# A fixed order of work in a token mix: first loads earlier, additions in pairs, outputs in one step

## The chip, the core and the metric

The kernel runs on one core of one Trainium2 chip. The metric is the device time of one execution in microseconds (us), from the runs of the kernel, with the program and its inputs unchanged between runs. One execution was also taken by the hardware profiler; its own time and its span stand in the table below.

Five engines work side by side, each through its own instructions in order: PE (matrix products), DVE (vector work), ACT (activations and copies), POOL (some copies, and one of the queues of DMA transfers) and SP (the main queue of DMA transfers). An instruction waits until the semaphores that it names have been raised by others; everything behind it on its engine waits with it.

## What is computed

The input is a sparse attention over 4 batches, 8 heads, 768 positions of 64 features, in blocks of 32 positions: each block of queries sees its neighbours, the first and the last block, and three sampled blocks; the first and the last block of queries see everything. Its result goes, heads side by side, as `x` (4 x 768 x 512) into a token mix:

```python
theta = x @ w_theta
cos_t, sin_t = (np.cos(theta), np.sin(theta))
zr = x * cos_t
zi = x * sin_t
yr = np.einsum('ts,bsd->btd', w_tok_r, zr)
yi = np.einsum('ts,bsd->btd', w_tok_i, zi)
y = yr + yi
u = x + y
return (u + np.maximum(u @ w_ch, 0.0)).astype(np.float32)
```

The weights come as 64-bit numbers and are decoded on the chip into a high and a low part (`w_theta_hi`, `w_ch_lo` and so on). Each product of two such values is made as three matrix products: high by high, high by low, low by high.

## The kernel before, in words

**Attention** (`attention`, up to about 290 us) runs over 56 units, one step of an outer loop for each; a unit is one block of queries of two batches with all heads (for the first and the last block: with a third of the keys). A step of that loop makes the scores of the next unit (L315, S), their maxima (L323, m), the exponentials (L341, P), transposes (L351, T; copied out at L357, pT), and the products with the values (L373, X) of the unit before, which DVE divides by their sums (L381 to L384, xo). SP stores the result to `xs` in DRAM (L400). The keys of a unit stand in `kg` (two places), its values in `va` and `vb`, its queries in `q` (four places, one for two units). Batches 0 and 1 of the mix are in the first half of `xs`, which attention has finished long before its last units.

**The mix** (`token_mix`) is a generator. Attention calls it in its last units, so that the first steps of the mix lie between them; the rest follows behind attention. The order inside is written out by hand and nothing reorders it: each engine gets its instructions as the code issues them. A step `k` of the mix takes 128 positions of one batch, six steps (`j` = 0 to 5) make a batch, 24 steps the whole. For a step there are:

- `load_raw` (L541) reads x of the step from `xs` into `xr` through SP's queue, `turn` (L553) transposes it on DVE into `xT`, `high` and `low` (L557 on ACT, L561 on DVE) split it, `theta` (L568 to L571) makes 12 products of 512 columns on PE;
- `integer` (L577, L578 on ACT) and `reduce` (L584 to L586 on DVE) bring the angle into range, `sines` (L592 to L594 on ACT) make cosine and sine, `load` (L535) reads x again as `xa`, in four transfers, `times` (L602 on DVE) multiplies, `split` (L609 on ACT, L610 on DVE) makes high and low parts `zh` and `zl`;
- `mix` (L627) makes 48 products: four groups `c` of 128 channels, each with a part of 512 positions in a bank of its own (`ya`, four banks) and a part of 256 positions; two groups share the bank of their smaller parts (`yb`, two banks);
- at `j` = 5 `add_x` (L642 on DVE) adds x to y, ACT copies the high part `uh` (L644) and DVE makes the low part `ul` (L645);
- the eight outputs of a batch (`out`, two column parts for each of four groups `e`; 12 products each at L651 to L653, sums in the two buffers of `ps_h`, which theta uses as well) are made in the middle of the mix of the next batch's steps `j` = 1 and `j` = 2, four in each; `finish` (L657 on DVE, into one of the two buffers `o`) adds, and L658 stores;
- the outputs of the last batch have no next step: `outs_at_the_end` makes them with sums in the banks of `ya` and `yb`, again two groups in one bank.

Step `k` issues, ahead of its own mix, theta of step `k`+2, sines, times and split of `k`+1, and turn, high and low of `k`+3. In the first eight steps pieces of the last weights are decoded as well, 14 in all by the list `shares`: a piece is ACT L62, DVE L67 to L77, ACT L80 (the high part), DVE L84 and L85 (the low part), and its raw words come through POOL's queue (L58) into one of two buffers. The last eight pieces are `w_ch`, the weights of the outputs.

SBUF places are taken by pools: the pools of the mix's later part (`xp` for xa, `tz` for sines, the decoder's, `zp` and so on) lie over those of attention, and the first write to a place waits for the last reader of what stood there. The bottom pool of attention is `gp`, which holds kg, va and vb together.

Of the kernel before, what the change touches and what calls it, by code (L numbers as in the profile page):

```python
# [19 lines left out]
P = 128  # L20
# [155 lines left out]
def attention(tc, qT, qE, kT, vr, sampled, xs, ident, early_pieces, late_pieces, first_place, follow):  # L176
# [13 lines left out]
    with ExitStack() as ctx, ExitStack() as early:  # L190
# [4 lines left out]
        ps_s = [early_s.enter_context(tc.tile_pool(name=f"ps_s{x}", bufs=1, space=PSUM, side="right")) for x in range(2)]  # L195
        gp = ctx.enter_context(tc.tile_pool(name="gp", bufs=1))
# [11 lines left out]
        kgs = [gp.tile([P, 8, 8, 32], F32, name=f"kg{x}") for x in range(2)]  # L208
# [223 lines left out]

        with tc.manual_schedule():
# [17 lines left out]
            for n in range(steps):  # L451
# [46 lines left out]
                if len(units) - 4 <= n < len(units):  # L498
                    next(follow)
# [3 lines left out]
def token_mix(tc, w, last_pieces, xs, outT, bias, nb):  # L503
# [11 lines left out]
    with ExitStack() as late, ExitStack() as ctx:  # L515
        tps = [ctx.enter_context(tc.tile_pool(name="tp0", bufs=1, side="right"))]
        hp = ctx.enter_context(tc.tile_pool(name="hp", bufs=2, side="right"))
        rp = ctx.enter_context(tc.tile_pool(name="rp", bufs=2, side="right"))
        ap = ctx.enter_context(tc.tile_pool(name="ap", bufs=1, side="right"))

# [92 lines left out]
        def mix(k, between):  # L613
# [4 lines left out]
            for c in range(4):  # L618
# [12 lines left out]
                if j == 5:  # L631
                    add_x(b, c)
# [4 lines left out]
        def add_x(b, c):  # L637
            if b not in us:
                us[b] = [up.tile([P, 4, 768], F32R, tag=f"u{x}", name=f"u{x}{b}") for x in "hl"]
            u = xT[b][:, c, :]  # L640
            for (t0, n), acc in zip(halves, ys[b][c]):
                nc.vector.tensor_tensor(u[:, t0 : t0 + n], acc, u[:, t0 : t0 + n], op=ALU.add)  # L642
            uh, ul = [t[:, c, :] for t in us[b]]
            nc.scalar.copy(uh, u)  # L644
            nc.vector.tensor_tensor(ul, u, uh.bitcast(F32), op=ALU.subtract)  # L645
# [9 lines left out]
        def finish(b, e, t0, n, ps, queue):  # L655
            o = wk.tile([P, 512], F32, tag="o", name=f"of{b}_{e}_{t0}")[:, :n]
            nc.vector.scalar_tensor_tensor(o, ps, 0.0, xT[b][:, e, t0 : t0 + n], op0=ALU.max, op1=ALU.add)  # L657
            queue.dma_start(outT[b, 128 * e : 128 * e + 128, t0 : t0 + n], o)  # L658

        def out(b, e, half):  # L660
            t0, n = half
            ps = ps_h.tile([P, 512], F32, tag="h", name=f"o{b}_{e}_{t0}")[:, :n]
            for c in range(4):
                channels(b, c, e, t0, n, ps, c == 0, c == 3)
            finish(b, e, t0, n, ps, nc.sync)

        def outs_at_the_end(b):
# [19 lines left out]
        load_raw(2)  # L687
# [27 lines left out]
        with tc.manual_schedule():  # L715
# [59 lines left out]
def sparse_attention_then_token_mix(ctx, tc, qT, qE, kT, vr, sampled, w_theta, w_tok_r, w_tok_i, w_ch, outT):  # L775
# [57 lines left out]
    follow = token_mix(tc, w, last, xs, outT, bias, n_batch)  # L833
    attention(tc, qT, qE, kT, vr, sampled.bitcast(I32), xs, ident, early, late, first_place, follow)
# [49 lines left out]
```

## Time and profile before

| what | us |
|---|---|
| runs of the kernel | 670.45, 670.45, 675.64 (median 670.45) |
| the profiled execution, its own time | 673.61 |
| its span, first to last instruction | 671.8 |
| PE busy | 564.7 (84%) |
| DVE busy | 425.7 (63%) |
| ACT busy | 327.3 (49%) |
| POOL busy | 148.2 (22%) |
| mean granted clock of PE | 0.946 of full speed |

In a timeline or chain row the first number is the start from the span's begin, the second the duration, both in us, then engine, line and operation; "x4" counts merged instructions; a bracket gives the idle time of the engine before it and what ended it. In a list of waits the three numbers are the total in us, how many times, and the longest. A matmul starts when the row says, but its duration reaches past the start of the next one: the distance between starts is what it takes.

### The profile page before, as it was taken

How to read it: one execution, taken by the hardware profiler on the slowest of the kernel's cores; microseconds unless marked ns; L12 is line 12 of the kernel's file. 1: busy time of each engine (PE TensorE's matmuls, PEld its weight loads, DVE VectorE, ACT ScalarE, POOL GpSimd, SP SyncE). 2: the span in 40 equal slices, each digit the busy share in tenths (PEclk: the TensorE clock that was granted, in tenths of full speed). 3: DMA queues.
4: the chain of work that ended last, by engine and by line, in shares of the span. 5: the costliest groups of instructions: out<-in, count | busy, mean ns of one | idle time of the engine just before them, and what ended most of it. 6: DMA issues, size and time to landing. Idle time of an engine off the chain costs nothing.

```text
span 671.8 us, 18527 instructions
## 1 busy us (share of the span) xinstructions
PE 564.7 (84%) x7648; PEld 443.5 (66%) x7648; DVE 425.7 (63%) x959; ACT 327.3 (49%) x660; POOL 148.2 (22%) x252
## 2 busy tenths in 40 slices
PE   2877666777878778779997978998999997999994
PEld 1554444555645456558886767887788886888873
DVE  4677657567899769649988784445743647543242
ACT  1866567556777758556554542243523344431110
POOL 1267445450396446130000000000000000000000
PEclk9988899889999889798998997998999999999998
DMA  8938999866789878642332122111111210111002
GB/s 321 302 91 239 283 269 260 234 181 237 220 234 283 242 214 251 183 126 80 90 94 79 33 77 78 66 47 33 35 67 63 72 47 18 46 48 48 0 1 94
DMA packets 57108, 90.47 MB, mean 135 GB/s; under 512 B 5696, under 2 KB 37568, under 8 KB 56640
## 3 DMA queue, kind: packets, MB, share of 16 engines
q1 hardware_dynamic: 47168, 57.02, 28.2%
q0 software_dynamic: 6688, 21.78, 12.2%
q10 hardware_dynamic: 3168, 10.49, 5.2%
q8 instruction: 60, 0.98, 0.6%
q14 instruction: 24, 0.20, 0.1%
HBM read 76.68 MB, written 12.58 MB: 133 GB/s over the span
## 4 chain that ended last, share of the span: by engine, by line
PE 50%; DVE 14%; DMA 3%; ACT 3%; issue 2%; POOL 0%; DVEq 0%; SPq 0%; ACTq 0%
PE ya L627 18%; PE yb L627 9%; PE h L568 3%; PE h L569 3%; PE h L571 3%; PE o L651 2%; PE o L652 2%; PE o L653 2%; DVE m L323 2%; DVE xT L642 2%; PE X L373 2%; PE S L315 1%; PE T L351 1%; DMA va<-in_vr_dram 1%; DMA xr<-xs 1%
## 5 line engine op out<-in xcount | busy, mean ns | idle before, releaser
L627 PE MATMUL ya<-w_second,zh 128*128 128x512 f32 x288 | 110.0, 404 | 0.0
L627 PE MATMUL yb<-w_second,zh 128*128 128x256 f32 x288 | 83.0, 288 | 14.8 <-DVE xT L642 14.8
L341 ACT ACTIVATE P<-S,nm 128x256 f32<-128x256 f32 x176 | 69.2, 480 | 16.8 <-DVE nm L325 15.9
L357 ACT COPY pT<-T 128x512 f32<-128x512 f32 x88 | 47.8, 591 | 48.3 <-PE T L351 46.8
L315 PE MATMUL S<-kg,q 64*32 64x256 f32 x1408 | 59.0, 412 | 14.7 <-issue 12.8
L323 DVE TENSOR_REDUCE m<-S 128x2 f32<-128x512 f32 x88 | 56.4, 683 | 20.7 <-PE S L315 20.6
L627 PEld LDWEIGHTS yb<-w_second,zh 128*128 128x128 f32 x288 | 56.0, 194 | 17.8 <-DVE xT L642 17.3
L373 PE MATMUL X<-va,pT 128*32 128x65 f32 (+1 forms) x1408 | 50.2, 234 | 20.3 <-issue 12.8
L351 PE MATMUL T<-ident,P 128*128 128x128 f32 x352 | 59.0, 299 | 8.7 <-ACT P L341 3.7
L627 PEld LDWEIGHTS ya<-w_second,zh 128*128 128x128 f32 x288 | 55.7, 193 | 13.9
L351 PEld LDWEIGHTS T<-ident,P 128*128 128x128 f32 x352 | 41.5, 148 | 33.4 <-ACT P L341 21.0
L627 PE MATMUL ya<-w_second,zl 128*128 128x512 f32 x144 | 58.9, 409 | 0.0
L373 PEld LDWEIGHTS X<-va,pT 128*32 128x32 f32 (+1 forms) x1408 | 35.8, 116 | 29.8 <-issue 18.4
L294 POOL DMA_INDIRECT vb<-in_vr_dram,rows x44 | 47.2, 1074 | 36.0 <-PE X_w L373 28.3
L373 PE MATMUL X<-vb,pT 128*32 128x65 f32 (+1 forms) x1408 | 49.9, 232 | 3.0 <-issue 3.0
L584 DVE SCALAR_TENSOR_TENSOR rr<-t,h 128x512 f32<-128x512 f32 x24 | 16.5, 688 | 45.1 <-ACT t L578 45.1
L315 PEld LDWEIGHTS S<-kg,q 64*32 64x32 f32 x1408 | 24.2, 112 | 31.2 <-issue 21.0
L373 PEld LDWEIGHTS X<-vb,pT 128*32 128x32 f32 (+1 forms) x1408 | 37.9, 117 | 5.5 <-issue 5.5
L627 PE MATMUL yb<-w_second,zl 128*128 128x256 f32 x144 | 41.3, 287 | 0.0
L627 PE MATMUL ya<-w_first,zh 128*128 128x512 f32 x96 | 36.9, 408 | 4.6 <-ACT zh L609 4.6
L657 DVE SCALAR_TENSOR_TENSOR of<-o,xT 128x512 f32<-128x512 f32 (+1 forms) x24 | 13.3, 558 | 43.4 <-PE o L653 43.4
L568 PE MATMUL h<-w_theta_hi,xh 128*128 128x512 f32 x96 | 39.3, 409 | 1.6 <-ACT xh L557 1.6
(165 smaller groups left out, 1280.4 us busy)
## 6 DMA issues: line engine op xcount, KB each, us to landing
va<-in_vr_dram SPq DMA_DIRECT2D x30, 260.0 KB
xr<-xs SPq DMA_DIRECT2D x24, 256.0 KB
q<-in_qT_dram SPq DMA_DIRECT2D x22, 256.0 KB
xs<-xo SPq DMA_DIRECT2D x44, 128.0 KB
xa<-xs SPq DMA_DIRECT2D x88, 64.0 KB
raw_tok_r<-in_w_tok_r_dram ACTq DMA_DIRECT2D x8, 576.0 KB
out_dram<-of SPq DMA_DIRECT2D x16, 256.0 KB
va<-in_vr_dram SPq DMA_DIRECT2D x30, 130.0 KB
```

The costliest lines, as they stand in the source:

```text
L294: nc.gpsimd.indirect_dma_start(out=vb[0:96], out_offset=None, in_=vr, in_offset=bass.IndirectOffsetOnAxis(ap=tab.rows[:, bp, i : i + 1], a ...
L315: nc.tensor.matmul(sc[32 * p : 32 * p + 32, e, b, :], q[rows, b, p, :], keys[rows, :, 4 * b + p, :], start=True, stop=True)
L323: nc.vector.tensor_reduce(m[:, 2 * e : 2 * e + 2], sc[:, e], axis=AX.X, op=ALU.max)
L341: nc.scalar.activation(pt[:, e, b], sc[:, e, b], AF.Exp, bias=nm[:, 2 * e + b : 2 * e + b + 1], scale=0.125)
L351: nc.tensor.transpose(banks[k // 4][:, k % 4], pt[:, (k // 2) % 2, k % 2, 128 * (k // 4) : 128 * (k // 4) + 128], ident)
L357: nc.scalar.copy(out[:, 4 * h : 4 * h + 4], bank)
L373: nc.tensor.matmul(s["X"][32 * p : 32 * p + 32, b, e, :], s["T"][0:rows, 4 * c + 2 * e + b, 32 * p : 32 * p + 32], v[0:rows, v0 : v0 + 65] ...
L568: nc.tensor.matmul(ps, hi[:, c, :], wh[:, c, :], start=c == 0, stop=False)
L569: nc.tensor.matmul(ps, hi[:, c, :], wl[:, c, :], start=False, stop=False)
L571: nc.tensor.matmul(ps, lo[:, c, :], wh[:, c, :], start=False, stop=c == 3)
L584: nc.vector.scalar_tensor_tensor(r, t, -C1, ps, op0=ALU.mult, op1=ALU.add)
L627: nc.tensor.matmul(acc, z[:, dd], wt[:, t0 : t0 + n], start=first and (n == 512 or c % 2 == 0), stop=last, skip_group_check=n == 256,)
```

## The change

Three things are changed, all in the written order and in the places of tiles.

**Loads.** The generator is called from the sixth unit before attention's end on (before: the fourth). Its first two calls only load the raw x of steps 0 and 1, into `spare` tiles that are places of the queries' pool `q`. The pools of the mix's first steps are taken by the third call, which loads step 2's x. The keys' places get a pool of their own, `kgp`, at the bottom, so that `xa` and the sines lie over keys alone, not over keys and values.

**Additions.** `add_x` is called behind the second group of a bank only, for both groups: the additions and high parts of the two, then the two low parts.

**Outputs.** All eight outputs of a batch are made in the mix of step `j` = 2. The decoded pieces are shared out as 2, 2, 1, 1, 2, 0, 2, 2, 2 over nine steps instead of 2, 2, 1, 1, 2, 1, 4, 1 over eight. At the end, one `finish` takes the two smaller parts of a bank together, 128 x 2 x 256, behind the second of them.

SP's queue at the end of attention, before: `xs<-xo_16` is the store of unit 16 of the second half, `xr` the raw x of steps 0, 1, 2, and `va` loads values.

```order
L400 DMA xs<-xo_16_5118 128x256
L288 DMA va_116<-in_vr_dram 64x1040
L400 DMA xs<-xo_17_5217 128x256
L288 DMA va_115<-in_vr_dram 32x1040 x2
L400 DMA xs<-xo_18_5307 128x256
L541 DMA xr_5327<-xs 128x4x128
L288 DMA va_116<-in_vr_dram 64x1040
L400 DMA xs<-xo_19_5405 128x256
L541 DMA xr_5410<-xs 128x4x128
L288 DMA va_115<-in_vr_dram 64x1040
L400 DMA xs<-xo_20_5497 128x256
L541 DMA xr_5505<-xs 128x4x128
```

The same place now:

```order
L401 DMA xs<-xo_16_5121 128x256
L540 DMA spare_5126<-xs 128x4x128
L289 DMA va_119<-in_vr_dram 64x1040
L401 DMA xs<-xo_17_5222 128x256
L540 DMA spare_5227<-xs 128x4x128
L289 DMA va_118<-in_vr_dram 32x1040 x2
L401 DMA xs<-xo_18_5314 128x256
L540 DMA xr_5334<-xs 128x4x128
L289 DMA va_119<-in_vr_dram 64x1040
L401 DMA xs<-xo_19_5412 128x256
L289 DMA va_118<-in_vr_dram 64x1040
L401 DMA xs<-xo_20_5502 128x256
```

Each of the three loads stands two stores, that is two units, further ahead.

DVE at the end of batch 0 (step 5), before: `yb_0` is the bank that groups 0 and 1 share, `yb_1` that of groups 2 and 3.

```order
L642 TENSOR_TENSOR xT_5412<-ya_0_5809,xT_5412 128x512
L642 TENSOR_TENSOR xT_5412<-yb_0_5807,xT_5412 128x256
L645 TENSOR_TENSOR ul_6403<-xT_5412,uh_6402 128x768
L642 TENSOR_TENSOR xT_5412<-ya_1_5810,xT_5412 128x512
L642 TENSOR_TENSOR xT_5412<-yb_0_5807,xT_5412 128x256
L645 TENSOR_TENSOR ul_6403<-xT_5412,uh_6402 128x768
L642 TENSOR_TENSOR xT_5412<-ya_2_5811,xT_5412 128x512
L642 TENSOR_TENSOR xT_5412<-yb_1_5808,xT_5412 128x256
L645 TENSOR_TENSOR ul_6403<-xT_5412,uh_6402 128x768
```

Now:

```order
L644 TENSOR_TENSOR xT_5417<-ya_0_5813,xT_5417 128x512
L644 TENSOR_TENSOR xT_5417<-yb_0_5811,xT_5417 128x256
L644 TENSOR_TENSOR xT_5417<-ya_1_5814,xT_5417 128x512
L644 TENSOR_TENSOR xT_5417<-yb_0_5811,xT_5417 128x256
L647 TENSOR_TENSOR ul_6406<-xT_5417,uh_6405 128x768 x2
L644 TENSOR_TENSOR xT_5417<-ya_2_5815,xT_5417 128x512
L644 TENSOR_TENSOR xT_5417<-yb_1_5812,xT_5417 128x256
L644 TENSOR_TENSOR xT_5417<-ya_3_5816,xT_5417 128x512
L644 TENSOR_TENSOR xT_5417<-yb_1_5812,xT_5417 128x256
L647 TENSOR_TENSOR ul_6406<-xT_5417,uh_6405 128x768 x2
```

The two readings of a bank now stand together, behind PE's products of both groups. PE's own order is the same there.

DVE at batch 0's outputs, before, from the last decoded piece (step 7) on; `of_0` to `of_3` are the finishes.

```order
L85 TENSOR_TENSOR w_ch_lo<-da_ch_6658,raw_ch_6542 128x256
L657 SCALAR_TENSOR_TENSOR of_0_0_6706<-o_0_0_6693,xT_5412 128x512
L657 SCALAR_TENSOR_TENSOR of_0_512_6722<-o_0_512_6709,xT_5412 128x256
L657 SCALAR_TENSOR_TENSOR of_1_0_6738<-o_1_0_6725,xT_5412 128x512
L657 SCALAR_TENSOR_TENSOR of_1_512_6754<-o_1_512_6741,xT_5412 128x256
L553 STREAM_TRANSPOSE xT_6111<-xr_6477 128x128 x4
```

Now, in step 8, again from the last decoded piece on:

```order
L85 TENSOR_TENSOR w_ch_lo<-da_ch_6759,raw_ch_6649 128x256
L660 SCALAR_TENSOR_TENSOR of_0_0_6807<-o_0_0_6794,xT_5417 128x512
L660 SCALAR_TENSOR_TENSOR of_0_512_6823<-o_0_512_6810,xT_5417 128x256
L660 SCALAR_TENSOR_TENSOR of_1_0_6839<-o_1_0_6826,xT_5417 128x512
L660 SCALAR_TENSOR_TENSOR of_1_512_6855<-o_1_512_6842,xT_5417 128x256
L660 SCALAR_TENSOR_TENSOR of_2_0_6871<-o_2_0_6858,xT_5417 128x512
L660 SCALAR_TENSOR_TENSOR of_2_512_6887<-o_2_512_6874,xT_5417 128x256
L660 SCALAR_TENSOR_TENSOR of_3_0_6903<-o_3_0_6890,xT_5417 128x512
L660 SCALAR_TENSOR_TENSOR of_3_512_6919<-o_3_512_6906,xT_5417 128x256
L552 STREAM_TRANSPOSE xT_6963<-xr_6597 128x128 x4
```

The finishes stand in one run behind step 8's own work and its two pieces; DVE's work for the step after comes behind all eight.

The diff, cut to its core:

```diff
@@ attention
+        kgp = ctx.enter_context(tc.tile_pool(name="kgp", bufs=1))
         gp = ctx.enter_context(tc.tile_pool(name="gp", bufs=1))
...
-        kgs = [gp.tile([P, 8, 8, 32], F32, name=f"kg{x}") for x in range(2)]
+        kgs = [kgp.tile([P, 8, 8, 32], F32, name=f"kg{x}") for x in range(2)]
...
+        spares.append(lambda: qp.tile([P, 4, 4, 32], F32, tag="q", name=f"spare{len(spares)}", bufs=Q_BUFS))
...
-                if len(units) - 4 <= n < len(units):
+                if len(units) - 6 <= n < len(units):
                     next(follow)
@@ token_mix
-        tps = [ctx.enter_context(tc.tile_pool(name="tp0", bufs=1, side="right"))]
-        hp = ctx.enter_context(tc.tile_pool(name="hp", bufs=2, side="right"))
-        rp = ctx.enter_context(tc.tile_pool(name="rp", bufs=2, side="right"))
-        ap = ctx.enter_context(tc.tile_pool(name="ap", bufs=1, side="right"))
...
-        def load_raw(k):
+        def load_raw(k, place=None):
 
             b, j = at(k)
-            xr[k] = rp.tile([P, 4, 4, 32], F32, tag="xr", name=f"xr{k}")
+            xr[k] = place() if place else rp.tile([P, 4, 4, 32], F32, tag="xr", name=f"xr{k}")
...
-                if j == 5:
+                if j == 5 and c % 2:
                     add_x(b, c)
...
-        def add_x(b, c):
+        def add_x(b, last):
             if b not in us:
                 us[b] = [up.tile([P, 4, 768], F32R, tag=f"u{x}", name=f"u{x}{b}") for x in "hl"]
-            u = xT[b][:, c, :]
-            for (t0, n), acc in zip(halves, ys[b][c]):
-                nc.vector.tensor_tensor(u[:, t0 : t0 + n], acc, u[:, t0 : t0 + n], op=ALU.add)
-            uh, ul = [t[:, c, :] for t in us[b]]
-            nc.scalar.copy(uh, u)
-            nc.vector.tensor_tensor(ul, u, uh.bitcast(F32), op=ALU.subtract)
+            uh, ul = us[b]
+            two = (last - 1, last)
+            for c in two:
+                for (t0, n), acc in zip(halves, ys[b][c]):
+                    part = xT[b][:, c, t0 : t0 + n]
+                    nc.vector.tensor_tensor(part, acc, part, op=ALU.add)
+                nc.scalar.copy(uh[:, c, :], xT[b][:, c, :])
+            for c in two:
+                nc.vector.tensor_tensor(ul[:, c, :], xT[b][:, c, :], uh[:, c, :].bitcast(F32), op=ALU.subtract)
...
-        def finish(b, e, t0, n, ps, queue):
-            o = wk.tile([P, 512], F32, tag="o", name=f"of{b}_{e}_{t0}")[:, :n]
-            nc.vector.scalar_tensor_tensor(o, ps, 0.0, xT[b][:, e, t0 : t0 + n], op0=ALU.max, op1=ALU.add)
-            queue.dma_start(outT[b, 128 * e : 128 * e + 128, t0 : t0 + n], o)
+        def finish(b, e, t0, n, ps, queue, groups=1):
+
+            o = wk.tile([P, 512], F32, tag="o", name=f"of{b}_{e}_{t0}")[:, : groups * n].rearrange("p (g t) -> p g t", g=groups)
+            nc.vector.scalar_tensor_tensor(o, ps, 0.0, xT[b][:, e : e + groups, t0 : t0 + n], op0=ALU.max, op1=ALU.add)
+            queue.dma_start(outT[b, 128 * e : 128 * (e + groups), t0 : t0 + n].rearrange("(g p) t -> p g t", g=groups), o)
...
-                        if c == 3:
-                            finish(b, e, t0, n, ps, nc.scalar if n == 256 else nc.sync)
-
-        load_raw(0)
+                        if c == 3 and n == 512:
+                            finish(b, e, t0, n, ps.unsqueeze(1), nc.sync)
+                    if c == 3 and e % 2:
+                        finish(b, e - 1, 512, 256, two[e // 2], nc.scalar, groups=2)
+
+        load_raw(0, spare)
         yield
-        load_raw(1)
+        load_raw(1, spare)
+        yield
+        tps = [ctx.enter_context(tc.tile_pool(name="tp0", bufs=1, side="right"))]
...
+        load_raw(2)
+        yield
         turn(0)
         yield
         high(0)
         low(0)
         yield
         turn(1)
-        load_raw(2)
         yield
...
-            shares = [2, 2, 1, 1, 2, 1, 4, 1]
+            shares = [2, 2, 1, 1, 2, 0, 2, 2, 2]
...
                 def outs():
-                    for _ in range(4 if j in (1, 2) else 0):
-                        if pending:
+                    if j == 2:
+                        while pending:
                             out(*pending.pop(0))
```

More of the change, by code (lines that the diff above doesn't have):

```diff
@@ L173, in make, with attention @@
         nc.vector.tensor_scalar(rows, base, ZEROS, None, op0=ALU.add)
-def attention(tc, qT, qE, kT, vr, sampled, xs, ident, early_pieces, late_pieces, first_place, follow):
+def attention(tc, qT, qE, kT, vr, sampled, xs, ident, early_pieces, late_pieces, first_place, follow, spares):
     nc = tc.nc
@@ L831, in last @@
         return pieces("tok_i", 3072, 4608, 256, chunks(second, 7, 2)) + pieces("ch", 0, 2048, 256, all_of("ch"))
-    follow = token_mix(tc, w, last, xs, outT, bias, n_batch)
-    attention(tc, qT, qE, kT, vr, sampled.bitcast(I32), xs, ident, early, late, first_place, follow)
+    spares = []
+    follow = token_mix(tc, w, last, xs, outT, bias, n_batch, lambda: spares[0]())
+    attention(tc, qT, qE, kT, vr, sampled.bitcast(I32), xs, ident, early, late, first_place, follow, spares)
     for _ in follow:
```

7 lines of the change are left out of this document (5 added, 2 removed).

## The prediction

> **What bounds the kernel now.** I read PE's waits first, from the mix's start to the end.
>
> ```profile
> PE yb L627 <- DVE xT L642: 14.8, 8, 4.6
> PE ya L627 <- ACT zh L609: 4.6, 1, 4.6
> PE o L651 <- DVE rr L584: 4.2, 1, 4.2
> PE ob L651 <- DVE of L657: 3.3, 1, 3.3
> PE o L651 <- DVE of L657: 1.7, 1, 1.7
> ```
>
> These are all of PE's waits behind 296 us. Elsewhere in the mix PE never waits, so only these gaps, what follows from them, and the mix's first product can move the end. What they cost in all shows in the chain, in order of time, at the last four products of each theta (L571), one per step:
>
> ```profile
> 313.23 0.93 PE h L571 x4
> ...
> 358.32 0.95 PE h L571 x4
> ...
> 418.97 0.93 PE h L571 x4
> ...
> 461.13 0.95 PE h L571 x4
> ...
> 477.87 0.93 PE h L571 x4
> 489.14 0.93 PE h L571 x4
> 508.76 0.93 PE h L571 x4
> ...
> 550.92 0.95 PE h L571 x4
> ...
> 566.16 0.93 PE h L571 x4
> ```
>
> An undisturbed step takes 489.14 - 477.87 = 11.27 us, and 508.76 - 489.14 = 19.62 with four outputs, so four outputs take 8.35. Of the 11.27, theta's 12 products are 2.81 (three times 0.93 and a little) and the mix is 8.46, 2.11 per group. In batch 0 the timeline has one theta that the chain passes by:
>
> ```profile
> 377.50 1.09 PE L571 MATMUL h<-w_theta_hi,xl 128*128 128x512 f32 x4
> ```
>
> Step 5, where batch 0 is added, takes 377.50 - 358.32 = 19.18, which is 7.91 over the rule. Steps 6 and 7 with the first four outputs take 418.97 - 377.50 = 41.47; 2 x 11.27 + 8.35 = 30.89, so 10.58 over. Batch 1's end (461.13 to 477.87) is 5.47 over, batch 2's (550.92 to 566.16) 3.97. That is more than the gaps, because PE can restart at half clock:
>
> ```profile
> 466.44 0.58 PE L627 MATMUL yb<-w_second,zh 128*128 128x256 f32 x1 [2.04 <-DVE xT L642]
> ...
> 556.23 0.38 PE L627 MATMUL yb<-w_second,zh 128*128 128x256 f32 x1 [2.04 <-DVE xT L642]
> ```
>
> ```profile
> 466.44:468.50 2.06, 2.06 (x6) 1.80 (x7) 0.96 (x1) 0.81 (x1) 0.00 (x0) 0.50 0.00 0
> ```
>
> The window row gives a granted clock of 0.50 behind the first gap. The second, equally long, was followed by short products: full clock.
>
> The mix's start is in the chain too, with DVE's two long waits there:
>
> ```profile
> 273.13 6.12 DMA xr<-xs
> ...
> 281.45 0.80 PE h L568
> ...
> 286.35 0.87 PE T L351 x8
> ...
> 291.26 1.10 PE X L373 x64
> ...
> 293.04 2.78 POOL xa L535 x4
> ...
> 298.54 0.70 DVE cs L602
> ...
> 299.93 0.79 PE ya L627
> ```
>
> ```profile
> DVE cs L602 <- DMA raw_tok_i<-in_w_tok_i_dram: 5.1, 1, 5.1
> DVE xT L553 <- DMA xr<-xs: 4.6, 1, 4.6
> ```
>
> The second of DVE's waits is booked on raw_tok_i, but the instruction reads xa, whose transfers started at 293.04, when the last values product was done: xa's place lay over values.
>
> **Part by part**, against the profiled execution's own 673.61 us (span 671.8), which is 3.2 above the median 670.45 of the runs.
>
> *Start: -9.6.* Step 0's load stood behind the store of unit 18 and landed 6.1 us later (273.13 to 279.25). Now it stands behind the store of unit 16:
>
> ```profile
> 264.46 0.35 SPq L400 DMA_DIRECT2D xs<-xo  x1
> ```
>
> 264.8 and 6.1 make 270.9, before DVE comes to the transpose:
>
> ```profile
> 274.69 0.42 DVE L384 TENSOR_TENSOR xo<-X,sm 128x256 f32<-128x256 f32 x1
> ```
>
> DVE is free at 275.1 and its wait of 4.6 goes. Late next is PE itself, which is at unit 20's values:
>
> ```profile
> 279.37 0.51 PE L373 MATMUL X<-vb,pT 128*32 128x65 f32 x8
> ```
>
> So theta 0 starts at 279.9 instead of 281.45. It took 4.9 us at half clock (to 286.35); with 1.6 us of idling gone I take 4.0, the end at 283.9, 2.4 earlier. Transposes, values and theta 1 follow as before, so the last values end at 292.4 - 2.4 = 290.0. The xa transfers wait for unit 22's scores only, whose keys they overlay; they go out near 276 behind POOL's last gather, and 5.5 us (293.04 to 298.54) put them down near 282. ACT's three sine steps, some 2 us, and the copy of xh (0.6) come before theta 2, which I put at 290.5 to 293.3. By then zh of step 0 is there, so the mix's first product starts at 293.3 instead of 299.93: -6.6. From first product to the next L571 row took 313.23 - 299.93 = 13.30 where full clock needs 8.46 + 2.81 - 0.93 = 10.34. PE no longer stands still before it, so these 2.96 go as well. Bounds: 2.4 (nothing behind theta 0 gained) and 4.6 + 5.1 + 3.0 = 12.7. The two spare loads pass two loads of values on SP's queue; the cover is that the code issues those two steps of its loop ahead of the values that use them. Should it fail, I put some 2 us of the gain at risk.
>
> *End of batch 0 and its outputs: 7.91 + 10.58 = 18.5 removed, 4.8 new, -13.7.* Additions now read a bank when PE has left it for good in this step; the bank is needed again after theta and, for the second one, half a mix: 2.8 and 7.0 us later. Of step 5's piece nothing is left to delay them. In exchange two pieces stand in step 8 ahead of its outputs. DVE's own work in a step and a piece:
>
> ```profile
> 378.52 0.88 DVE L553 STREAM_TRANSPOSE xT<-xr 128x128 f32<-128x128 f32 x4
> ...
> 384.46 0.29 DVE L67 TENSOR_SCALAR da_ch<-da_ch 128x256 f32<-128x256 f32 x1
> ...
> 387.04 0.29 DVE L67 TENSOR_SCALAR da_ch<-da_ch 128x256 f32<-128x256 f32 x1
> ```
>
> That is 5.94 and 2.58; with two pieces 11.1, just under PE's 11.27. The additions and low parts of the second pair stand behind step 5's last product:
>
> ```profile
> 371.73 0.96 DVE ul L645
> 372.69 0.94 DVE xT L642 x2
> ```
>
> A pair of additions is 0.94, a low part 0.96. One and a half such pairs (the first large part can be read earlier) and two low parts, 3.3, is what DVE lags PE by when step 6 begins, and with 11.1 per step it stays so. In step 8, counted from its start, PE reaches the outputs at 2.81 + 4.23 = 7.0; it needs the first of the two pieces for the last group of the first output, at 7.0 + 2.1 = 9.1, and gets it at 3.2 + 5.94 + 2.58 = 11.7: a delay of 2.1. The third output needs a sum buffer that the first finish empties, behind the second piece: 14.3 + 0.7 = 15.0 against 13.4, 1.6 more. To these 3.7 I add 1.0 for the clock, half of the 2.0 that four us at half clock cost, since the rows at 466.44 and 556.23 show one of each. Bounds: 18.5 with no new delay; 7.9 if the outputs wait as long as before.
>
> [...]
>
> *Ends of batches 1 and 2: -5.5 and -4.0.* All of the excess goes; DVE decodes nothing there, and the cover is the same 2.8 and 7.0 us. With DVE 3 us late it would still hold. Eight outputs in a row on two buffers cost what four and four did. Bounds: nothing, and all.
>
> *End of batch 3: -2.2*, its share of the eight waits, in 630 to 645 us:
>
> ```profile
> PE yb L627 <- DVE xT L642: 2.2, 2, 1.5
> ```
>
> *Last outputs: -2.1.* They are bound not by PE but by the two buffers `o`, each of which has to be stored before it is filled again:
>
> ```profile
> 659.07 0.69 DVE L657 SCALAR_TENSOR_TENSOR of<-oa,xT 128x512 f32<-128x512 f32 x1 [10.55 <-PE oa L653]
> ...
> 661.91 0.69 DVE L657 SCALAR_TENSOR_TENSOR of<-oa,xT 128x512 f32<-128x512 f32 x1 [1.82 <-PE ob L653]
> ...
> 664.75 0.69 DVE L657 SCALAR_TENSOR_TENSOR of<-oa,xT 128x512 f32<-128x512 f32 x1 [1.82 <-DMA out_dram<-of]
> ...
> 668.19 0.41 DVE L657 SCALAR_TENSOR_TENSOR of<-ob,xT 128x256 f32<-128x256 f32 x1
> ```
>
> One round of a buffer is 2.84. Eight results are four rounds, six are three. On the same time axis the second buffer now starts one group of PE later (8.35 / 8 = 1.04), at 660.1, and its third finish runs from 660.1 + 5.7 = 665.8 to 666.5, against 668.6. The last store is twice as large; its price is in no row alone, and since a round with the large size is 2.84 I take nothing (bounds: 0 and 2.4 gained). The 3.3 wait of PE goes into this and is not counted twice.
>
> Sum: 9.6 + 13.7 + 5.5 + 4.0 + 2.2 + 2.1 = 37.1, so 636.5 against the profiled execution and 633.3 against the median. I take 635.
>
> **Rivals.**
>
> *The second wait at the start stays* (POOL or the places hold xa back, or the sines are late). For it: xa of step 1 still stands behind raw_tok_i, which waits for the last values. Against: step 0's xa does not. It leaves 2.4 of 9.6: 643.7.
>
> *Batch 0's outputs wait as long as before*, since all pieces now end right ahead of them. For it: DVE runs at 11.1 of 11.27 through steps 6 to 8. Against: 3.7 is what the rows give. 10.58 instead of 4.8: 642.3.
>
> *The additions' wait is moved, not removed*: the next batch's first products need the same banks and wait for both groups' additions. Against: 2.8 and 7.0 us of cover, with 1.9 of additions for a pair of groups (two rows like that at 372.69). It takes back 5.5 + 4.0 + 2.2 + 7.9: 656.1.
>
> *Slower*: in the runs of eight outputs PE stops at every buffer, and the clock stays at half. Then each run of 16.7 costs 16.7 more, 50 in three batches: 686.6. It decides from the point where finish and store of one buffer (2.84) take longer than two outputs on PE (4.18). The four-output run at 489 to 508 shows no pause, which is against it. [...]
>
> **How the numbers follow.** Chances: forecast 0.65; second wait stays 0.13; outputs wait 0.12; additions' wait moved 0.04; several at once, ending near no change, 0.03; slower 0.03. The least and the most of the forecast's terms and the first two rivals, from either of the two starting times, reach from about 628 to 649; that is the range, and leaves out the third rival and what is behind it. One per cent (6.7 us) is about what a measurement of this kernel can tell from no change: faster by over 1% takes the first four cases, 0.94; within 1% 0.03; slower 0.03.
>
> **What would show it.** Right: no wait of DVE's first transpose on a transfer, and the first mix product right behind theta 2; no wait of `yb` on an addition in the middle of a mix; at 11.27 between thetas at all ends of batches; in step 8 one or two waits of `o` near 2 us; six finishes at the end with rounds of 2.8. Wrong: first product more than 3 us behind theta 2; waits on additions at the first products of steps 6, 12, 18; a granted clock of 0.5 through outputs; attention's last values later than 290.

## The result, and the profile after

The changed kernel takes 635.06 us (median of 4 runs, 631.24 to 640.28) where the kernel before takes 672.65 in the same measurement (670.45 to 675.64); the ratio is 0.944 with the interval 0.936 to 0.953. The prediction was 635 (628 to 649), faster by over 1% with a chance of 0.94. The profiled execution took 634.94 (span 633.2) against 673.61 (span 671.8): 38.6 of span, where the sum of the prediction was 37.1. Medians are of all runs; the ratios leave out runs that took over 1.5% longer than the fastest of their kernel, such as the one of 687.21 in e4.

The same view that was read first before, PE's waits from the start of the mix, now has three rows, four stops in all, each of them in the outputs in step 8 (line numbers moved by a few with the change):

```profile
PE o L653 <- DVE of L660: 2.2, 2, 1.3
PE o L653 <- ACT w_ch_hi L80: 2.0, 1, 2.0
PE o L655 <- DVE w_ch_lo L85: 0.4, 1, 0.4
```

The waits on additions, on `zh` at the start and on the result buffers at the end are gone. Where the time went is read best between four marks that both kernels have: the store of attention's unit 18, and the first of the four low products of theta 3, theta 11 and theta 23. Start, duration and name in the timelines of the kernel before:

```profile
272.69 0.34 SPq L400 DMA_DIRECT2D xs<-xo  x1
...
313.07 1.09 PE L571 MATMUL h<-w_theta_hi,xl 128*128 128x512 f32 x4
...
438.42 1.10 PE L571 MATMUL h<-w_theta_hi,xl 128*128 128x512 f32 x4
...
616.49 1.10 PE L571 MATMUL h<-w_theta_hi,xl 128*128 128x512 f32 x4
```

and of the changed one, with its first mix product:

```profile
272.60 0.34 SPq L401 DMA_DIRECT2D xs<-xo  x1
...
290.92 0.39 PE L626 MATMUL ya<-w_first,zh 128*128 128x512 f32 x1
...
301.26 1.09 PE L570 MATMUL h<-w_theta_hi,xl 128*128 128x512 f32 x4
...
413.85 1.10 PE L570 MATMUL h<-w_theta_hi,xl 128*128 128x512 f32 x4
...
582.53 1.09 PE L570 MATMUL h<-w_theta_hi,xl 128*128 128x512 f32 x4
```

The four stages between these marks, for both kernels and for all experiments below (us; each from one profile, so made in the same way):

| kernel | unit 18 to theta 3 (start) | theta 3 to 11 (batch 0) | theta 11 to 23 (batches 1, 2) | theta 23 to the end | span |
|---|---|---|---|---|---|
| before | 40.4 | 125.4 | 178.1 | 55.3 | 671.8 |
| after | 28.7 | 112.6 | 168.7 | 50.6 | 633.2 |
| difference (forecast) | -11.7 (-9.6) | -12.8 (-13.7) | -9.4 (-9.5) | -4.7 (-4.3) | -38.6 (-37.1) |
| e1 loads only | 27.9 | 125.2 | 176.5 | 55.3 | 658.1 |
| e2 additions only | 39.5 | 118.3 | 168.6 | 52.6 | 647.5 |
| e3 outputs only | 39.7 | 115.3 | 178.3 | 55.3 | 659.7 |
| e4 last results only | 40.1 | 125.2 | 177.8 | 53.3 | 667.9 |
| e5 keys under again | 35.6 | 110.8 | 168.7 | 50.6 | 637.1 |
| e6 x loaded late | 33.1 | 111.1 | 168.7 | 50.6 | 634.2 |
| e7 outputs later | 29.5 | 106.9 | 168.5 | 50.6 | 633.0 |
| e8 places for results | 30.3 | 111.8 | 168.7 | 47.8 | 626.5 |
| e10 both | 31.0 | 107.3 | 168.5 | 47.8 | 626.1 |
| after, again | 28.3 | 113.7 | 168.7 | 50.6 | 633.9 |

A stage without any wait is known from the prediction's rule: eight steps with eight outputs are 8 x 11.27 + 16.7 = 106.9, and twelve steps with sixteen outputs 12 x 11.27 + 33.4 = 168.6. So the changed kernel loses nothing in the two middle batches and 5.7 in batch 0. The changed kernel, e7, e8 and e10 have the same instructions ahead of unit 18, and yet that store starts anywhere from 267.99 (e8) to 277.48 (e7): attention wanders by nearly 10 us from run to run, about as much as the whole times of one kernel do (631.24 to 640.28). The start, from unit 18 to theta 3, wanders by 3 us among the kernels that share it (27.9 to 31.0); the stages behind it repeat to about a microsecond, apart from the half clock (0.50 for 6.83 us in step 8 of the second profile of the changed kernel, 1.00 in the first).

**Start.** x of step 0 is there when DVE comes to it. xa goes out at 276.08, when PE has done the last scores (274.22 to 275.31), and no longer behind the last values (up to 287.6). Theta 0 runs at full clock (1.00 granted from 278.92 to 281.50, 0.39 for a product; in the kernel before 0.59 from 281.45 to 286.35, 0.63 for a product):

```profile
275.23 0.89 DVE L552 STREAM_TRANSPOSE xT<-spare 128x128 f32<-128x128 f32 x4
...
276.08 2.78 POOL L534 DMA_DIRECT2D xa<-xs  x4 [3.47 <-PE T L352]
...
278.92 0.39 PE L568 MATMUL h<-w_theta_lo,xh 128*128 128x512 f32 x1
```

**Step 8.** PE stops four times in the outputs. PE's timeline, with the idle time and its releaser in brackets, and DVE's beside it:

```profile
387.16 0.39 PE L655 MATMUL o<-uh,w_ch_lo 128*128 128x512 f32 x1
389.55 0.50 PE L653 MATMUL o<-uh,w_ch_hi 128*128 128x512 f32 x1 [2.00 <-ACT w_ch_hi L80]
389.89 0.39 PE L654 MATMUL o<-ul,w_ch_hi 128*128 128x512 f32 x1
390.70 0.50 PE L655 MATMUL o<-uh,w_ch_lo 128*128 128x512 f32 x1 [0.41 <-DVE w_ch_lo L85]
...
393.88 0.49 PE L653 MATMUL o<-uh,w_ch_hi 128*128 128x512 f32 x1 [1.25 <-DVE of L660]
...
399.23 0.50 PE L653 MATMUL o<-uh,w_ch_hi 128*128 128x512 f32 x1 [0.93 <-DVE of L660]
```

```profile
392.80 0.42 DVE L85 TENSOR_TENSOR w_ch_lo<-da_ch,raw_ch 128x256 fp32r<-128x256 f32 x1
393.14 1.02 DVE L660 SCALAR_TENSOR_TENSOR of<-o,xT 128x512 f32<-128x512 f32 x2
398.49 1.02 DVE L660 SCALAR_TENSOR_TENSOR of<-o,xT 128x512 f32<-128x512 f32 x2 [4.33 <-DMA out_dram<-of]
```

The first two stops wait for the first of step 8's two pieces, the third for a finish behind the second piece. The fourth waits for a finish that itself waits for a result buffer, whose store was issued at 393.85 and took 4.5 us. The granted clock stayed full in this stretch (a row of the windows: length, busy time of PE, its loads, DVE, ACT and POOL, then granted clock, share of DMA and GB/s):

```profile
388.00:404.00 16.00, 11.85 (x65) 9.89 (x66) 7.77 (x21) 2.92 (x6) 0.00 (x0) 1.00 0.18 62
```

**End.** Six finishes; the third to sixth each wait for a store:

```profile
625.19 0.69 DVE L660 SCALAR_TENSOR_TENSOR of<-ob,xT 128x512 f32<-128x512 f32 x1 [1.07 <-DMA out_dram<-of]
626.24 0.69 DVE L660 SCALAR_TENSOR_TENSOR of<-oa,xT 128x512 f32<-128x512 f32 x1 [0.35 <-DMA out_dram<-of]
628.16 0.69 DVE L660 SCALAR_TENSOR_TENSOR of<-oa,xT 128x512 f32<-128x512 f32 x1 [1.24 <-DMA out_dram<-of]
629.06 0.69 DVE L660 SCALAR_TENSOR_TENSOR of<-ob,xT 128x512 f32<-128x512 f32 x1 [0.20 <-DMA out_dram<-of]
```

### The profile page after: what moved, and what is told of

Read it like the earlier page. It is cut to its first block, busy times and chain, and to the rows that moved or that the text cites. A ratio compares the mean times of both kernels' runs of the same rounds, so it can differ in the third digit from the quotient of the medians.

```text
span 633.2 us, 18520 instructions
## 1 busy us (share of the span) xinstructions
PE 555.6 (88%) x7648; PEld 437.1 (69%) x7648; DVE 426.1 (67%) x957; ACT 326.6 (52%) x660; POOL 146.2 (23%) x252
## 3 DMA queue, kind: packets, MB, share of 16 engines
q1 hardware_dynamic: 47168, 57.02, 30.3%
## 4 chain that ended last, share of the span: by engine, by line
PE 45%; DVE 15%; ACT 5%; DMA 3%; issue 3%; POOL 1%; DVEq 0%; ACTq 0%
PE ya L626 14%; PE yb L626 7%; PE X L374 3%; PE T L352 3%; PE S L316 3%; PE h L567 2%; PE o L653 2%; PE h L570 2%; PE o L654 2%; PE h L568 2%; PE o L655 2%; ACT zh L608 2%; DMA out_dram<-of 1%; DVE m L324 1%; DMA va<-in_vr_dram 1%
## 5 line engine op out<-in xcount | busy, mean ns | idle before, releaser
L626 PE MATMUL ya<-w_second,zh 128*128 128x512 f32 x288 | 107.1, 396 | 0.0
L626 PE MATMUL yb<-w_second,zh 128*128 128x256 f32 x288 | 80.5, 279 | 0.0
L342 ACT ACTIVATE P<-S,nm 128x256 f32<-128x256 f32 x176 | 69.0, 477 | 15.7 <-DVE nm L326 12.4
L374 PE MATMUL X<-va,pT 128*32 128x65 f32 (+1 forms) x1408 | 50.3, 228 | 17.1 <-issue 12.7
L352 PE MATMUL T<-ident,P 128*128 128x128 f32 x352 | 57.7, 298 | 7.7 <-ACT P L342 4.0
L374 PE MATMUL X<-vb,pT 128*32 128x65 f32 (+1 forms) x1408 | 54.9, 226 | 11.0 <-issue 9.6
L626 PEld LDWEIGHTS ya<-w_second,zh 128*128 128x128 f32 x288 | 54.1, 188 | 14.0
L626 PEld LDWEIGHTS yb<-w_second,zh 128*128 128x128 f32 x288 | 54.4, 189 | 0.4
L374 PEld LDWEIGHTS X<-vb,pT 128*32 128x32 f32 (+1 forms) x1408 | 39.9, 113 | 14.6 <-issue 14.3
L316 PEld LDWEIGHTS S<-kg,q 64*32 64x32 f32 x1408 | 25.6, 110 | 23.8 <-issue 13.8
L568 PE MATMUL h<-w_theta_lo,xh 128*128 128x512 f32 x96 | 37.8, 394 | 0.0
```

Source lines behind the costliest of these rows:

```text
L316: nc.tensor.matmul(sc[32 * p : 32 * p + 32, e, b, :], q[rows, b, p, :], keys[rows, :, 4 * b + p, :], start=True, stop=True)
L342: nc.scalar.activation(pt[:, e, b], sc[:, e, b], AF.Exp, bias=nm[:, 2 * e + b : 2 * e + b + 1], scale=0.125)
L352: nc.tensor.transpose(banks[k // 4][:, k % 4], pt[:, (k // 2) % 2, k % 2, 128 * (k // 4) : 128 * (k // 4) + 128], ident)
L374: nc.tensor.matmul(s["X"][32 * p : 32 * p + 32, b, e, :], s["T"][0:rows, 4 * c + 2 * e + b, 32 * p : 32 * p + 32], v[0:rows, v0 : v0 + 65] ...
L568: nc.tensor.matmul(ps, hi[:, c, :], wl[:, c, :], start=False, stop=False)
L626: nc.tensor.matmul(acc, z[:, dd], wt[:, t0 : t0 + n], start=first and (n == 512 or c % 2 == 0), stop=last, skip_group_check=n == 256,)
```

## The experiments

First each of the change's four parts alone on the kernel before, to see whether the terms of the sum are each part's own.

### e1: the loads alone

```diff
+        kgp = ctx.enter_context(tc.tile_pool(name="kgp", bufs=1))
...
-                if len(units) - 4 <= n < len(units):
+                if len(units) - 6 <= n < len(units):
...
-        load_raw(0)
+        load_raw(0, spare)
...
```

> The kernel before with the loads part alone: x of steps 0 to 2 loaded earlier, into places of queries, keys in a pool of their own. Theory (the start is worth what stands in the trace of the changed kernel, and PE is the bound behind it, so the gain is kept to the end): the first mix product near 291 us instead of 299.9, no half clock behind it, together 12 us off: 661.7 against the profiled execution's 673.6, a ratio of 0.982. Excess at the ends of the batches as before (7.9 and 10.6, 5.5, 4.0). Rival: batch 0 is paced by DVE's decoding and its loads, not by PE, and gives most of it back at the end of batch 0: 668 to 674.

Measured: 659.26 us, ratio 0.979 (0.975 to 0.983). The start took 27.9 (-12.4), batch 0 125.2 (-0.1), so nothing is given back there; the rival falls. The 1.5 in the middle batches is put down to the clock, by an estimate: both pauses of 2.03 and 2.04 passed without half clock here (1.00 granted from 454.3 to 460.0 and from 542 to 546), where the kernel before was granted 0.50 for 3.41 us from 466.40, and half of 3.41 is 1.7 (see the last section).

### e2: the additions alone

```diff
-                if j == 5:
+                if j == 5 and c % 2:
                     add_x(b, c)
...
```

(`add_x` as in the change.)

> The kernel before with the additions of y behind both groups of a bank, nothing else. Theory: all waits of the second halves in the middle of a mix go, and with them the half clock: 7.9 + 5.5 + 4.0 + 2.2 = 19.6 off: 654.0 against 673.6, ratio 0.971. The 10.6 of the first four outputs of batch 0 stay, since four pieces still stand ahead of them. Rival: with the piece in step 5 still ahead of the additions (2.58) DVE is some 6 us behind when step 6 begins, more than the cover of 2.8, and the first products of step 6 wait some 3 us: 657 or more. Second rival: the waits move to the first products of every batch: 665.

Measured: 655.96 us, ratio 0.976 (0.972 to 0.980). The profiled execution took 649.3, but 4.2 of that is attention ahead of unit 18. By stages it is -7.0, -9.4 and -2.7, together 19.2 before rounding, of the expected 19.6. PE's waits behind the first mix product are these, and none is on an addition or at the first products of a batch:

```profile
PE o L654 <- DVE rr L584: 4.2, 1, 4.2
PE ob L654 <- DVE of L660: 3.3, 1, 3.3
PE o L654 <- DVE of L660: 1.4, 1, 1.4
PE o L654 <- ACT w_ch_hi L80: 1.2, 1, 1.2
PE o L656 <- DVE w_ch_lo L85: 0.4, 1, 0.4
```

Both rivals fall: the pairs of additions are done before their banks are needed, even with a decode piece ahead of them. The waits of batch 0's outputs stay, as expected.

### e3: the outputs and the shares alone

```diff
-            shares = [2, 2, 1, 1, 2, 1, 4, 1]
+            shares = [2, 2, 1, 1, 2, 0, 2, 2, 2]
...
-                    for _ in range(4 if j in (1, 2) else 0):
-                        if pending:
+                    if j == 2:
+                        while pending:
```

> The kernel before with all eight outputs of a batch in one step and the shares 2,2,1,1,2,0,2,2,2, nothing else. Theory: the outputs of batch 0 cost 5.7 over the rule, as in the changed kernel, instead of 10.6 (-4.9), and the additions of batch 0 no longer stand behind a piece, so the first wait falls from 4.6 to 2.0 (-2.6): 666.1 against 673.6, ratio 0.989. Rival: the runs of eight outputs stop PE at every buffer and lose the clock: slower than 673.6. Second rival: with the additions still cut apart DVE reaches step 8 later than in the changed kernel, and nothing of the 4.9 comes: 671.

Measured: 660.09 us, ratio 0.980 (0.976 to 0.985). Batch 0 gave 10.0, more than the 7.5 expected: 4.1 at the end of step 5, because the pause of 4.61 that shrank to 2.04 had also cost half clock (0.50 granted from 364.00 to 370.83 before, 1.00 from 361.3 to 364.5 in e3), and 5.9 at the outputs. The kernel before had run those at half clock for 10 us behind its stop of 4.24:

```profile
401.55:411.79 10.24, 8.55 (x29) 7.14 (x28) 4.78 (x12) 2.18 (x4) 0.00 (x0) 0.50 0.15 52
```

In e3 the stops there are 0.79, 0.41, 1.24 and 0.96, together 3.40; with 0.27 for each restart, as in step 8 of the changed kernel, that is an estimated 4.5, all that is left of the 10.4 before, so nothing remains for half clock. Twelve steps with sixteen outputs took 178.3 against 178.1, so eight outputs in a row cost no more than four and four, and "slower" falls.

The stages of e2 and e3 in batch 0 are -7.0 and -10.0, together -17.1, while the whole change has -12.8. The overlap is step 5: e2 takes 8.1 out of it (19.35 to 11.27 between its two thetas), and the 4.1 that e3 takes out of it are part of these 8.1.

### e4: the last results alone

```diff
...
-                        if c == 3:
-                            finish(b, e, t0, n, ps, nc.scalar if n == 256 else nc.sync)
+                        if c == 3 and n == 512:
+                            finish(b, e, t0, n, ps.unsqueeze(1), nc.sync)
+                    if c == 3 and e % 2:
+                        finish(b, e - 1, 512, 256, two[e // 2], nc.scalar, groups=2)
```

> The kernel before with the last eight results in six finishes, nothing else. Theory: three rounds of the two result buffers instead of four, with the second one started 1 us later: 2.1 off, from the last mix product to the end; ratio 0.997. Rival: the last store, twice as large, takes the gain back: no difference. In both, PE's wait of 3.3 us on a result (ob behind a finish) goes or stays without moving the end by itself.

Measured: 669.45 us, ratio 0.993 (0.989 to 0.996). The last stage is 53.3 against 55.3: -2.0, for 2.1. So the store of double size takes back next to nothing (0.1).

### e5 and e6: the two waits of the start, one at a time

In e5 the keys lie in the pool of the values again; the loads stay early.

```diff
-        kgp = ctx.enter_context(tc.tile_pool(name="kgp", bufs=1))
...
-        kgs = [kgp.tile([P, 8, 8, 32], F32, name=f"kg{x}") for x in range(2)]
+        kgs = [gp.tile([P, 8, 8, 32], F32, name=f"kg{x}") for x in range(2)]
```

> The changed kernel with the keys put back into the pool of the values, so that xa of step 0 lies over values again; the early loads into places of queries stay. Theory (the pool of keys is what lets xa go out): theta 0 starts early as in the changed kernel (near 278.6), but xa goes out only behind the last values product (287.7) and the first mix product comes 7.5 us behind that, near 295.2 instead of 290.9; behind such a pause PE starts at half clock, 3.0 more: 7.3 slower than the changed kernel's 634.9, so 642.2. Rival: what held xa back was its place in POOL's queue, not the memory: no difference, 635.

In e6 the keys' pool stays, and x of steps 0 and 1 is loaded behind the store of unit 18.

```diff
-        load_raw(0, spare)
         yield
-        load_raw(1, spare)
         yield
+        load_raw(0, spare)
         ...
+        load_raw(1, spare)
         yield
         turn(0)
```

> The changed kernel with x of steps 0 and 1 loaded into the same places, but behind the store of unit 18, where the kernel before loads step 0; keys in their own pool. Theory: DVE's first transpose waits for the transfer again (about 4 us), theta 0 starts near 281 and at half clock, and all behind it comes 4 us later: 639.0 against 634.9; no second pause ahead of the first mix product. Rival: with xa there in time the values of the last units cover the wait: 635.

Measured: e5 640.78 us, e6 636.34 (two runs each). The start took 35.6 and 33.1, which is 6.9 and 4.4 more than in the changed kernel; expected were 7.3 and 4.1. In e5 xa went out only behind the last values, and PE paused for 4.76 and restarted at half clock (0.50 granted from 294.6 to 298.6, a product of 512 columns at 0.63 or above). POOL's wait is booked on ACT's first sine step, which itself had waited for the values: its place lies over them too, and this run does not tell the two places apart. ACT's timeline, POOL's and PE's:

```profile
286.94 0.63 ACT L590 ACTIVATE cs<-rr 128x512 f32<-128x512 f32 x1 [0.39 <-PE X L373]
```

```profile
287.60 2.79 POOL L533 DMA_DIRECT2D xa<-xs  x4 [16.88 <-ACT cs L590]
```

```profile
294.63 0.79 PE L625 MATMUL ya<-w_first,zh 128*128 128x512 f32 x1 [4.76 <-ACT zh L607]
295.22 0.41 PE L625 MATMUL yb<-w_first,zh 128*128 128x256 f32 x1
295.44 0.63 PE L625 MATMUL ya<-w_first,zh 128*128 128x512 f32 x1
```

In e6 DVE's wait for x came back, and the one for xa did not (DVE's waits):

```profile
DVE xT L552 <- DMA spare<-xs: 5.0, 1, 5.0
```

So the two measures are independent, as far as the 3 us by which the start wanders let one tell: 40.4 falls to 35.6 with early x alone, to 33.1 with early xa alone, and 4.8 + 7.3 = 12.1 is about the 11.7 of both. Neither shows in full in the whole time: e5 and e6 lose 1.8 and 1.4 less in batch 0 than the changed kernel, since PE comes later to step 8 while DVE's decoding isn't later by as much. PE's stops in step 8 add up to 3.1 and 2.2 instead of 4.6: the first is 1.4 and 1.8 instead of 2.0, the fourth is gone in both and the third in e6, where half clock takes part of it back (from 392.95 to 395.46 a product of 512 columns took 0.79 and one of 256 columns 0.41, for 0.50 and 0.28 in the changed kernel).

### e7: what step 8's waits are worth

The eight outputs of batch 0 are put behind the last group of step 8, 4.23 us later on PE.

```diff
-                if c == 1:
+                if c == (3 if k == 8 else 1):
                     between()
```

> The changed kernel with the eight outputs of batch 0 behind the last group of step 8 instead of behind its second, 4.23 us later on PE; the same instructions otherwise. Theory (the outputs wait only for the two pieces and the finishes that stand behind them on DVE): all waits of step 8 go, 4.6 of waits and 1.1 of clock: 629.2 against 634.9. Rival: the result buffers, whose stores took 4.5 us there, bind by themselves: 1 to 2 of it stay. Second rival: theta 11 and z of step 9 stand behind outputs and wait instead: 635.

Measured: batch 0 took 106.9, as much as with no wait at all, and PE's waits behind the first mix product are an empty list; -5.7 against the changed kernel, as expected. The fourth stop went too: the finishes now come one by one as PE delivers (398.61, 399.62, 402.41), not two at once behind a piece. The whole time, 633.54 (627.21 to 634.81), doesn't tell it from the changed kernel; in the profiled run unit 18 was stored 4.9 later than there.

### e8: what the end's waits are worth

```diff
+            room = [None, None, tile(tz, "cs", 0, bufs=2), tile(tz, "cs", 1, bufs=2), tile(ap, "rr", 2), tile(tz, "rr", 3)]
...
-                            finish(b, e, t0, n, ps.unsqueeze(1), nc.sync)
+                            finish(b, e, t0, n, ps.unsqueeze(1), nc.sync, place=room.pop(0))
```

> The changed kernel with the last six results in six places of their own (two are the result buffers, four are buffers of sines and angles that are free by then), so that no finish waits for a store. Theory: the last finish ends near 626.6, right behind PE's last product, instead of 629.75: 3.1 less, 631.8 against 634.9. Rival: the stores share the way to memory and take longer when they come together: 1 or less.

Measured: 630.85 us (628.3 to 640.16); the last stage is 47.8 against 50.6: -2.9, for 3.1. No finish waits for a store. The last two finishes follow PE directly:

```profile
621.73 0.69 DVE L660 SCALAR_TENSOR_TENSOR end<-oa,xT 128x512 f32<-128x512 f32 x1 [0.21 <-PE oa L655]
622.34 0.68 DVE L660 SCALAR_TENSOR_TENSOR end<-ob,xT 128x512 f32<-128x512 f32 x1
```

From the last finish's start to the end of the span it is 4.1, as in the changed kernel (633.2 - 629.06), so the last store took no longer for coming closer behind the others.

### e10 and the changed kernel beside it

> The changed kernel with both: the outputs of batch 0 behind the last group of step 8, and the last six results in six places. Theory: the two gains are in different stages and add, 5.7 + 3.1: 626.1 where the changed kernel has 634.9; from the first mix product to the end 333.5 where the changed kernel has 342.3. Rival: the end is the same work in the same order, and the gain of the end comes back as stores in a queue: 629.

> The changed kernel once more beside it, on the same chip, to compare the two: 635, and from the first mix product to the end 342, since attention ahead of it wanders from run to run and the mix does not. Rival: the 342 were a single profile's luck with the clock in step 8: 340 or 344.

Measured side by side: both edits together 627.76 us (ratio to before 0.940, 0.934 to 0.946), the changed kernel 636.40 (0.954, 0.948 to 0.959). From the first mix product to the end it is 626.1 - 292.09 = 334.0 and 633.9 - 290.70 = 343.2. The gains add, and this version beats both kernels, the changed one by 1.4%. The mix of the changed kernel repeats to about 1 us (342.3 and 343.2), but not by the same path. Here three stops (2.23, 0.41 and 0.55) add up to 3.2 us instead of 4.6, and behind the first two of them PE runs at half clock, which the first profile did not have in step 8 (1.00 from 388.00 to 404.00):

```profile
391.46:398.29 6.83, 6.28 (x20) 5.02 (x19) 2.45 (x7) 2.18 (x4) 0.00 (x0) 0.50 0.17 60
```

## Why the prediction was right, term by term

- **The bound.** "Elsewhere in the mix PE never waits, so only these gaps, what follows from them, and the mix's first product can move the end" held: the stages without waits are 168.5 to 168.7 in every kernel that has the additions behind pairs, whatever else was changed, and what the start saves (e1) reaches the end.
- **Start, -9.6: measured -11.7; the mis-sized term.** The step that fell short is theta 0: "4.9 us at half clock ... I take 4.0", from 279.9. It started at 278.58 and took 3.0 at full clock, 1.3 and 1.0 better. All behind it came as told: the first mix product 2.4 earlier than forecast (290.92 for 293.3), xa out at 276.08 for "near 276", 10.34 from the first mix product to theta 3 (13.13 before by the timeline alone; the prediction's 13.30 ends in a row of the chain). The 1.3 is not fully the change's: PE's own stop at unit 20's values, which the trace books on nothing, was 1.57 before and 0.52 here, but 1.60 in e7. Over the six profiles with this start the gain is 9.4 (e10) to 12.4 (e1), so the forecast lies at the low end of what the start wanders by.
- **Batch 0, -13.7: measured -12.8.** 18.5 removed and 4.8 new was forecast, 5.7 new came. The 18.5 is right, but its two parts were each taken between a row of the chain and one of the timeline, whose starts lie 0.17 apart: by the timeline alone they are 8.08 and 10.41. The two waits told, 2.1 and 1.6, were 2.4 and 1.25; by the prediction's own numbers the first is 11.7 - 9.1 = 2.6, which leaves 1.1 for the second, and the sum of 3.7 stays. Not foreseen was the fourth stop (0.93, a store of 4.5 us). And the 1.0 "for the clock" was right by chance. No run shows the four us at half clock that it was worked out from: behind the pause that ended at 466.44 it was 3.41, and in step 8 the granted clock was 1.00 in this profile, and half for 6.83 us in the second one. What took its place is that each of the four stops cost more than its idle time. The product behind it took 0.50 (0.49 once) instead of 0.39, and the next started 0.34 behind it (0.33 once) instead of 0.23; with the gap ahead counted from the end of a product that overlaps its successor (0.39 long, 0.23 apart), the rows at 387.16 to 389.89 give 389.89 - 387.16 = 2.73 where 0.46 would do, 2.27 for an idle time of 2.00. Four stops are 4.59 of idle and 4 x 0.27 = 1.1. The same holds for what went: PE's four waits in the 18.5 are 4.61, 0.93, 4.24 and 1.69, together 11.5; of the other 7.0, half clock is 6.6 by an estimate (PE was busy for 4.63 us from 366.20 to 370.83 and for 8.55 from 401.55 to 411.79, both granted 0.50), which leaves 0.4 for restarts.
- **Batches 1 and 2, -9.5: measured -9.4.** The cover of 2.8 and 7.0 held. The rival that the additions' wait is only moved is refuted by e2.
- **End, -4.3: measured -4.7**, of which the additions are 2.7 (e2) and the six finishes 2.0 (e4), for 2.2 and 2.1.
- **Rivals.** "The second wait at the start stays" would have cost what e5 shows, 6.9 at the start (the prediction had 7.2): it was a real danger, and the keys' pool is what keeps it away. "Outputs wait as before" and "slower" have nothing for them in the profile after.

635 was taken between 636.5 (against the profiled execution) and 633.3 (against the median). The whole times of the two kernels spread over 0.8% and 1.4% from run to run, so 635 against 635.06 is closer than the method can be; the stages are what bears it out.

## To carry to other kernels

Where one engine has no idle time outside a few gaps, cost each gap as the difference between the spacing of a repeating instruction and its undisturbed spacing, not as the idle time in the list of waits: that takes in the clock and the restart (the first stop of step 8 was 2.27 so, for an idle time of 2.00). Which pool a tile shares decided when its transfer could go out: with the keys in the pool of the values xa went out at 287.60, with a pool of their own at 276.08, and the list of waits named a sine step, not the values (e5). A consumer that comes a few microseconds too early can be moved later within the same step (e7: 4.23 us later, 5.7 gained) instead of hurrying its producer, and a round of too few buffers at the end can borrow those that are no longer used (e8: 2.9 gained).

## What was not expected of the hardware

- **Equal pauses, unequal clock.** Pauses of 2.03 or 2.04 us on PE, all at the same place of a mix, are in the profiles of before, e1, e3 and e4, and the clock granted behind them was not the same. It was 0.50 behind the one that ended at 466.44 before (at once, to 469.81), behind the one that ended at 454.11 in e3 (about 1.4 us later: 0.89 from 454 to 456, 0.50 from 456 to 459) and in e4 from 553.8 to 556.3. It was 1.00 behind the one that ended at 556.23 before (556 to 560), in e1 from 454.3 to 460.0 and from 542 to 546, in e3 from 361.3 to 364.5 and in e4 from 464.7 to 468.0. In the kernel before the two differ in where they lie. From 270 us to the last outputs its trace has half clock in five stretches, of 6.83, 6.83, 6.83, 10.24 and 3.41 us, and the full clock between them in stretches of 13.65, 58.03, 30.72 and 54.61: all are whole multiples of 3.41. Cut into pieces of 3.41 on these borders, the time from 300 to 590 us has three pieces at full clock in which PE was idle for 2.00 us or more (2.41 to 364.00, 3.08 to 401.55, 2.00 to 466.40), each with 0.50 behind it; in its other pieces at full clock PE was idle for 1.32 us at most, and 1.00 followed. The pause that ended at 466.44 lies in one piece, which leaves 1.41 of PE's time in 3.41; the one that ended at 556.23 is split between two, and no half clock follows. The kernel before, at both:

```profile
462.99:466.40 3.41, 1.41 (x9) 0.95 (x7) 2.74 (x5) 0.56 (x1) 0.00 (x0) 1.00 0.00 0
466.40:469.81 3.41, 3.37 (x11) 2.89 (x12) 0.96 (x1) 0.83 (x1) 0.00 (x0) 0.50 0.02 5
...
551.73:555.14 3.41, 2.46 (x14) 1.86 (x12) 1.71 (x3) 1.41 (x2) 0.00 (x0) 1.00 0.00 1
555.15:558.56 3.41, 2.33 (x14) 2.08 (x15) 2.27 (x5) 0.83 (x1) 0.00 (x0) 1.00 0.00 0
```

  This is read from the profiles afterwards; no run here was made to test it. The two profiles of the changed kernel lie on either side: in step 8 the first has 1.73 us of idle time from 385.86 to 389.27 and full clock behind it, the second 1.77 from 388.05 to 391.46 and half clock. Behind four longer pauses PE restarted at half clock: 0.50 from 299.93 to 305.97 behind 4.62 us and from 366.20 to 370.83 behind 4.61 us before, 0.50 from 294.6 to 298.6 behind 4.76 us in e5, and 0.53 from 355 to 361 behind 5.6 us in e1.
- **Restart.** The stops of PE at full clock cost about 0.27 us each beyond their idle time (four stops in step 8; the two stops of 2.04 and 1.48 at the end of batch 2 of the kernel before, 3.52 of idle and 3.97 of time, say 0.23 each).
- **Stores that land late.** A store of a result took 1.97 us at the end and 4.51 in step 8 (393.85 to 398.37), although DMA was nearly idle in the second half of it: 262 GB/s in the microsecond from 395, 2 in the next, 11 on the mean from 396.0 to 398.3. A result buffer in step 14 came back after about 4 us as well (its finish ended at 488.52, the next into it began at 492.65). So two buffers, with a finish each 1.4 to 2.8 us, were just enough in step 14 (1.11 us of waiting on DVE, none on PE), and not in step 8, where finishes came two at once. What such a store waits for isn't in these traces.
